# FNet and gated layers on one core: opening statistics moved between engines, two twin pairs for turning, and a stretch without tests

## The chip, the core and the metric

The kernel runs on one core of a Trainium2 chip. The metric is the device time of one execution in microseconds; the median of the runs counts. Engines are named as the profile names them: PE is TensorE's matmuls and PEld its weight loads, DVE is VectorE, ACT is ScalarE, POOL is GpSimd, SP is SyncE, whose queue issues nearly every DMA.

## The reference

Two rounds of two layers on x of 2048 rows and 640 columns. The first layer adds the real part of a two-dimensional DFT of the normalised rows, the second a gated product with hidden width 1728 (w_gate, w_up and w_down are drawn eight times larger than the function below it says):

```python
def _A_ref(x, dft_seq_re, dft_seq_im, dft_hid_re, dft_hid_im):
    a = jnp.einsum("bsd,ed->bse", x, dft_hid_re)
    b = jnp.einsum("bsd,ed->bse", x, dft_hid_im)
    return jnp.einsum("ts,bse->bte", dft_seq_re, a) - jnp.einsum("ts,bse->bte", dft_seq_im, b)
def _B_ref(x, w_gate, w_up, w_down):
    g = jnp.einsum("bsd,df->bsf", x, w_gate)
    u = jnp.einsum("bsd,df->bsf", x, w_up)
    return jnp.einsum("bsf,fd->bsd", _sigmoid(g) * u, w_down)
x = x + _A_ref(_layernorm(x), ...)
x = x + _B_ref(_layernorm(x), w_gate, w_up, w_down)
x = x + _A_ref(_layernorm(x), ...)
x = x + _B_ref(_layernorm(x), w_gate, w_up, w_down)
```

## The kernel before, in words

**The folded DFT.** The DFT matrices have mirror symmetry, and `folded` uses it: rows s and S-s, and s and S/2-s, are added and subtracted first, so that the sequence product is taken over a quarter of the rows. x stands in SBUF as four blocks (0 to 3) of four groups A, B, C, D of 128 rows; the groups B and C run backwards and have to be turned. `turn_round` (L349-352) does that on PE with a reversal matrix, two matmuls of 320 columns into a pair of PSUM banks called a twin; `turned` (L354-357) copies the twin back to SBUF on ACT and takes the sum of each row on the way. Four twins use all eight PSUM banks, and `drop_twins` gives these to the matmuls, as eight `acc` banks, once the last twin has been copied.

**Statistics.** The layer norm's mean and variance of each row come in two ways: by DVE's batch statistics (L415, L416), or on ACT. ACT's way is a sum, then a square of x minus the mean with the sum of the squares (`turned_squares`, L363-365, for B and C; `fold_stats_act`, L571-575, for five groups of A and D). For the square, POOL first makes the mean from the sum (`turned_means`, L361); afterwards POOL divides the squares' sum (`square_means`, L373), and `rstd_power` adds eps (L398) and takes the power -1/2 (L399), also on POOL. `rstd_step` (L401-408) then does a Newton step, in the opening on DVE, five small operations, and `fold_scale` (L600-613) makes the coefficients from it.

**Folds.** `fold_columns` (L578-585) adds and subtracts the column halves of a group pair on DVE, `fold_double` (L587-595) doubles column 0 (L590) and, for block 1, copies a single row (L595), `zero_odd` (L838-841) clears two columns, `fold_rows` (L615-630) scales the rows on ACT (L624, L626) and DVE (L630), and `fold_join` (L645-660) adds the four groups on DVE. `sequence32` (L802-822) is the first sequence DFT in fp32 on PE. A call takes its banks one after the other; `seq 0 1` stands first and has three chains.

**What sets the order.** Each engine runs its instructions in the order in which they are emitted. Until PE has its first down projection's operands, that order is the list `OPENING` (L156-178), written out by hand: "turn i g", "turned i g", "stats i g", "means i", "square i g", "smeans i", "power i", "scale i", "col i k", "double i k", "zero i", the row products "re", "ro", "de", "do", "join i e" and "join i o", "seq i tp", and so on, each word one call for block i (the dictionary `todo`, L1615-1645). Later the PE programme (`steps`) is run in order, each step with a planned duration; `when(t, f)` calls f at the planned time t, between steps. Memory is given out in slots by the table `PLACES` (L74-111), in the order in which it is taken.

**The second block of the gated layer.** Layer 0's rows are done in two halves. While PE runs the first half's down projection (L1299), the second half is normalised in four pairs of row tiles: ACT applies the norm (L442), DVE combines pairs (L492-495), ACT and DVE make f16 parts (L507, L508), and an SP transpose DMA (L524) turns them into PE's operand. The gate and up products (L1157) start when the last transpose has landed.

**Other work beside it.** The folding holds only if the DFT matrices have the symmetry. 100 tests check that while the layers run: each loads a tile of the matrix (L1485, mostly four DMAs on SP), compares on DVE (L1492, L1494) and sums squares on ACT (L1464); a flag sends the program to `general` if one fails. They are spread by `spans`: stretches of the plan with a weight, in which tests stand at even distances (4.704 planned us over the weight). Besides, `load_c`, `split_c` and `keep_c` (L702-730) load blocks of the DFT matrix again, split them into f16 parts (L236 on ACT, L238 on DVE) and store them for layer 1; L1059 to L1068 make sums of weights, and `load_s` (L1086 to L1092) loads the first products' weights.

## Time and profile before

| What | us |
|---|---|
| median of three runs (1130.19 to 1132.08) | 1131.68 |
| the profiled execution | 1127.54 |
| its span, first to last instruction | 1125.7 |
| PE busy in the span | 1089.4 |
| DVE busy | 834.2 |
| ACT busy | 571.7 |
| POOL busy | 153.7 |

The mean granted clock of the profiled execution was 0.988. The lines that matter are shown with the prediction. A line of the waits reads: engine, tile and line that waited, what released it, total us, times, longest. A line of the timeline reads: start, us, engine, line, operation, output from input and their shape, count, and in brackets the idle time before it with its releaser. A line of the groups reads: line, engine, operation, count, busy us, mean ns, and idle time before. A line of the windows gives for each engine the busy time and the count of instructions that started, then the granted clock of PE in parts of full speed and the mean busy share of the DMA engines.

### The profile page before, as it was taken

To read this page: it belongs to the slowest core of one execution; us is meant where nothing else is said; L and a number is where in the kernel's file an instruction comes from. 1 tells how busy PE (TensorE), PEld (TensorE's weight loads), DVE (VectorE), ACT (ScalarE), POOL (GpSimd) and SP (SyncE) were. 2 spreads that over 40 slices of the span, in tenths; PEclk is the share of its full clock that TensorE was granted. 3 is DMA by queue.
4 is the path that set the end of the run, shared out by engine and by line. 5 is a ranking of instruction groups with operands and counts; after the bars stand their busy time and mean duration, and the time that the engine had idled before them with its cause. 6 is when DMAs were issued, how large, how long until landed. Compare 5 with 4: busy or idle time off the path is not lost.

```text
span 1125.7 us, 17470 instructions
## 1 busy us (share of the span) xinstructions
PE 1089.4 (97%) x6279; PEld 621.4 (55%) x6279; DVE 834.2 (74%) x1623; ACT 571.7 (51%) x1108; POOL 153.7 (14%) x241
## 2 busy tenths in 40 slices
PE   5899999999997999999999999999999999999997
PEld 3667444447773444447777754444667444444775
DVE  7887589959385999858786659886796356767962
ACT  6776447856152556546224544477654245554520
POOL 3200131421322433100020100002000010000010
PEclk8899999999998999999999999999999999999999
DMA  8312674365989776856833027645668965655621
GB/s 280 140 36 69 189 231 148 124 187 165 232 226 293 254 212 226 235 172 201 239 87 133 1 47 180 191 148 172 203 158 175 232 220 176 224 184 179 201 84 62
DMA packets 183080, 194.69 MB, mean 173 GB/s; under 512 B 76459, under 2 KB 145476, under 8 KB 182984
## 3 DMA queue, kind: packets, MB, share of 16 engines
q1 hardware_dynamic: 182344, 190.86, 57.5%
q0 software_dynamic: 640, 2.62, 0.6%
q8 instruction: 51, 0.84, 0.3%
q14 instruction: 45, 0.37, 0.1%
HBM read 145.29 MB, written 31.90 MB: 157 GB/s over the span
## 4 chain that ended last, share of the span: by engine, by line
PE 79%; DVE 9%; DMA 4%; issue 3%; SPq 2%; POOL 2%; ACT 1%; DVEq 0%; POOLq 0%; ACTq 0%
PE acc L1157 39%; PE acc L1413 14%; PE acc L1113 14%; PE acc L907 4%; PE acc L819 2%; DMA big<-in_wu 2%; PE acc L1394 2%; PE acc L1266 2%; DVE big L238 1%; DMA big<-big 1%; DVE big L1287 1%; DVE big L508 1%; SPq L1485 1%; PE acc L776 1%; SPq L524 1%
## 5 line engine op out<-in xcount | busy, mean ns | idle before, releaser
L1157 PE MATMUL acc<-big 128*128 128x512 f16 x2160 | 469.0, 380 | 10.4 <-issue 7.9
L1157 PEld LDWEIGHTS <-big 128*128 128x128 f16 x2160 | 211.5, 98 | 266.6 <-issue 12.9
L1413 PE MATMUL acc<-big 128*128 128x320 f16 x1512 | 213.5, 299 | 2.5 <-DVE big L1287 2.5
L1161 ACT ACTIVATE big<-acc 128x512 f32<-128x512 f32 x160 | 94.2, 594 | 197.2 <-PE acc L1157 191.6
L1413 PEld LDWEIGHTS <-big 128*128 128x128 f16 x1512 | 147.9, 98 | 60.9 <-issue 3.1
L1113 PE MATMUL acc<-big 128*128 128x512 f16 (+1 forms) x900 | 156.3, 336 | 0.0
L1113 PEld LDWEIGHTS <-big 128*128 128x128 f16 x900 | 87.9, 98 | 67.6 <-issue 0.3
L1464 ACT ACTIVATE big<-big 128x768 f32<-128x768 f32 (+6 forms) x106 | 78.9, 745 | 51.7 <-DVE big L1494 21.2
L238 DVE SCALAR_TENSOR_TENSOR big<-big 128x640 f16<-128x640 f32 (+8 forms) x94 | 75.5, 826 | 26.1 <-ACT big L236 26.1
L1374 DVE TENSOR_TENSOR big<-big 128x512 f16<-128x512 f32 x126 | 84.5, 682 | 7.6 <-ACT big L1373 7.6
L1299 PE MATMUL acc<-big 128*128 128x320 f16 x656 | 89.3, 299 | 0.0
L1287 DVE SCALAR_TENSOR_TENSOR big<-acc,big 128x320 f32<-128x320 f32 x112 | 53.1, 484 | 42.6 <-PE acc L1394 24.6
L1373 ACT ACTIVATE big<-big 128x512 f16<-128x512 f32 x126 | 72.8, 617 | 18.6 <-DVE big L1251 7.9
L236 ACT ACTIVATE big<-big 128x640 f16<-128x640 f32 (+9 forms) x94 | 63.2, 706 | 30.9 <-DMA big<-in_ct 14.2
L1299 PEld LDWEIGHTS <-big 128*128 128x128 f16 x656 | 64.2, 98 | 25.1
L1207 DVE TENSOR_TENSOR big<-big,acc 128x512 f32<-128x512 f32 x40 | 27.2, 680 | 46.3 <-ACT big L1464 23.2
L1164 ACT ACTIVATE big<-big 128x512 f32<-128x512 f32 x80 | 49.7, 621 | 6.5 <-DVE big L1207 6.4
L507 ACT ACTIVATE big<-big 128x384 f16<-128x384 f32 (+2 forms) x56 | 36.5, 666 | 31.9 <-DVE big L492 17.1
L379 POOL DMA_INDIRECT out<-big,rows x8 | 9.0, 1121 | 312.0 <-DVE big L1287 164.8
L1385 DVE TENSOR_TENSOR big<-big 128x512 f32<-128x512 f32 x72 | 49.6, 691 | 0.1
L1492 DVE TENSOR_TENSOR big<-big 128x512 f32<-128x512 f32 x64 | 45.3, 707 | 4.6 <-DMA big<-in_ct 4.6
L907 PE MATMUL acc<-big 128*128 128x321 f16 (+3 forms) x324 | 48.5, 300 | 0.0
(193 smaller groups left out, 1196.0 us busy)
## 6 DMA issues: line engine op xcount, KB each, us to landing
big<-in_ct SPq DMA_DIRECT2D x256, 128.0 KB
big<-kept_f SPq DMA_DIRECT2D x63, 320.0 KB
big<-kept_S SPq DMA_DIRECT2D x33, 512.0 KB
big<-kept_w SPq DMA_DIRECT2D x33, 320.0 KB
big<-in_ct SPq DMA_DIRECT2D x32, 256.0 KB
big<-kept_G SPq DMA_DIRECT2D x21, 320.0 KB
kept_S<-big SPq DMA_DIRECT2D x13, 512.0 KB
big<-in_wg SPq DMA_DIRECT2D x19, 320.0 KB
```

Source lines behind the costliest of these rows:

```text
L236: nc.scalar.activation(dh, src, AF.Copy, scale=s)
L238: nc.vector.scalar_tensor_tensor(dl, src, s, dh, op0=OP.mult, op1=OP.subtract)
L907: nc.tensor.matmul(ps[:m, :EC], z[:, at : at + m], w[:, 384 * wp : 384 * wp + EC], start=(d == 0 and zp == HI and wp == HI), stop=(d == ND ...
L1113: nc.tensor.matmul(ps, w[wp][:, d * P : (d + 1) * P], xt[:, xp, :], start=(d == 0 and wp == HI and xp == HI), stop=(d == ND - 1 and wp == LO))
L1157: nc.tensor.matmul(ps, wt, xt, start=start and n == 0, stop=n == len(todo) - 1, skip_group_check=not start)
L1161: nc.scalar.activation(dst, ps, AF.Copy)
L1287: nc.vector.scalar_tensor_tensor(xe, ps[:, :EH], CB, xe, op0=OP.mult, op1=OP.add)
L1299: nc.tensor.matmul(held["pd", i, e][0][:, :EH], held["t", half, j].parts[hp][:, i * P : (i + 1) * P], held["w", 2, j].parts[wp][:, e * EH ...
L1373: nc.scalar.activation(h, v, AF.Copy)
L1374: nc.vector.tensor_tensor(l, v, h, op=OP.subtract)
L1413: nc.tensor.matmul(ps[:, :EH], a[n][hp][:, i * P : (i + 1) * P], w[n][:, wp], start=fresh and m == 0, stop=m == len(todo) - 1, skip_group_ ...
L1464: nc.scalar.activation(v, v, AF.Square, accum_out=new_sum()[:p])
```

## The change

It has five parts. Line numbers of the new kernel are one to five higher than those above.

1. **Who does the small operations of the opening.** ACT's squares take the raw sum as bias and -640 as scale, so they need no mean; the variance's factor becomes 1/D³ (`square_means`, now on DVE). POOL still makes the means, now also those of ACT's A and D groups. Adding eps goes from POOL to DVE and only the power stays on POOL; `rstd_step` on DVE has four operations for five. `fold_double` with its row copies goes from DVE to POOL while the opening lasts, and `zero_odd`'s memset too. Later, `norm_stats_act` is scaled in the same spirit, and `npow`'s eps goes to DVE.
2. **PSUM.** Two twins in place of four, one for B and one for C; the other four banks are `acc` banks from the start, and `drop_twins` adds four more.
3. **The list `OPENING`** is written anew, and with it the table `PLACES`.
4. **Tests.** The first span of the tests is split in two, with nothing between 38 and 76 us (of the plan) behind the start of layer 0's first down projection. With this the distance is 4.607 planned us over the weight.
5. **Layer 1's blocks of the DFT matrix** are loaded, split and stored from 96 planned us on, 11.5 apart, and no longer from 104 on, 13.5 apart.

```diff
 PLACES = """
-224 171 112 387 160 267 284 290 314 401 250 137 166 153 344 100 374 381 331 257 340 85 364 132 260 349 94 80
...
+305 80 399 324 195 319 369 208 352 246 286 400 130 100 81 105 125 153 269 121 156 374 346 273 262 143 116 159
...
 OPENING = """
-    turn 0 B, stats 0 A, turn 0 C, turned 0 B, turned 0 C, turn 1 B, stats 0 D, means 0, square 0 C, col 0 0,
-    turn 1 C, double 0 0, stats 1 A, turned 1 B, square 0 B, smeans 0, zero 0, col 0 1, turned 1 C, stats 1 D,
-    col 1 0, power 0, stats 2 D, turn 2 B, turned 2 B, turn 3 C, double 1 0, turn 2 C, double 0 1, col 1 1, means 1,
-    square 1 C, scale 0, col 2 0, wld 4 0, zero 1, re 0 0, turn 3 B, ro 0 0, turned 3 C, de 0 0, square 1 B,
-    double 1 1, ro 0 1, do 0 0, smeans 1, re 0 1, power 1, col 3 1, turned 2 C, stats 2 A, do 0 1, de 0 1, zero 2,
-    join 0 o, means 2, scale 1, join 0 e, double 2 0, square 2 C, ro 1 1, square 2 B, col 2 1, re 1 0, smeans 2,
...
+    turn 0 B, wld 4 0, stats 0 A, turned 0 B, turn 0 C, turn 1 B, square 0 B, turned 0 C, stats 0 D, col 0 0,
+    square 0 C, wld 3 0, means 0, col 0 1, smeans 0, turned 1 B, double 0 0, square 1 B, turn 1 C, zero 0, turn 2 B,
+    stats 1 D, turned 1 C, double 0 1, square 1 C, power 0, turn 2 C, col 1 0, turned 2 B, stats 1 A, means 1,
+    smeans 1, scale 0, double 1 0, stats 2 A, re 0 0, re 0 1, power 1, turned 2 C, ro 0 1, ro 0 0, stats 2 D,
+    col 1 1, square 2 B, turn 3 B, col 2 0, de 0 1, scale 1, square 2 C, de 0 0, do 0 0, col 2 1, row 0, zero 2,
+    smeans 2, means 2, turn 3 C, ro 1 0, join 0 e, ro 1 1, double 1 1, re 1 1, do 0 1, do 1 0, power 2, double 2 0,
...
     big = pool.tile([P, UNITS * UNIT], F32, name="big")
-    acc = []
+    psum = ctx.enter_context(tc.tile_pool(name="ps", bufs=1, space=bass.MemoryType.PSUM))
+    acc = [psum.tile([P, 512], F32, name=f"acc{i}") for i in range(4)]
     flag = pool.tile([P, 1], I32, name="flag")
...
     X = big[:, : XU * UNIT].rearrange("p (r c) -> p r c", c=D)
-    banks = []
+    banks = list(range(4))
     minus = pool.tile([P, 4], F32, name="minus")
...
     room_of = turning.__enter__()
-    twins = [room_of.tile([P, 2, 512], F32, name=f"twin{k}") for k in range(4)]
+    twins = [room_of.tile([P, 2, 512], F32, name=f"twin{k}") for k in range(2)]
...
     def twin(i, g):
-        return twins[(2 * i + (g == GC)) % 4]
+        return twins[g == GC]
...
     def drop_twins():
         turning.__exit__(None, None, None)
-        pool8 = ctx.enter_context(tc.tile_pool(name="ps", bufs=1, space=bass.MemoryType.PSUM))
-        acc.extend(pool8.tile([P, 512], F32, name=f"acc{i}") for i in range(8))
-        free_bank(*range(8))
+        rest = ctx.enter_context(tc.tile_pool(name="ps4", bufs=1, space=bass.MemoryType.PSUM))
+        acc.extend(rest.tile([P, 512], F32, name=f"acc{i}") for i in range(4, 8))
+        banks.extend(range(4, 8))
...
     def load_x(i, g):
...
-    def turned_means(i):
+    def sums_to_means(i):
         t = quad_tile(i)
-        nc.gpsimd.tensor_scalar(t[:, GB:GD, 12], t[:, GB:GD, 20], 1.0 / D, None, op0=OP.mult)
+        g0, g1 = GB - ((i, GA) in ON_ACT), GD + ((i, GD) in ON_ACT)
+        nc.gpsimd.tensor_scalar(t[:, g0:g1, 12], t[:, g0:g1, 20], 1.0 / D, None, op0=OP.mult)
...
     def turned_squares(i, g):
         t = quad_tile(i)
-        nc.scalar.activation(held["xr", i, g].f32, X[:, 4 * i + g, :], AF.Square, bias=t[:, g, 12:13], scale=-1.0,
+        nc.scalar.activation(held["xr", i, g].f32, X[:, 4 * i + g, :], AF.Square, bias=t[:, g, 20:21], scale=-float(D),
                              accum_out=t[:, g, 22:23])
...
         g0, g1 = GB - ((i, GA) in ON_ACT), GD + ((i, GD) in ON_ACT)
-        nc.gpsimd.tensor_scalar(t[:, g0:g1, 13], t[:, g0:g1, 22], 1.0 / D, None, op0=OP.mult)
+        nc.vector.tensor_scalar(t[:, g0:g1, 13], t[:, g0:g1, 22], 1.0 / D**3, None, op0=OP.mult)
...
     def store_x(i, g, c):
...
     def rstd_step(t, n, to, on=nc.gpsimd, times=-1.0):
...
         on.tensor_tensor(c[16], c[14], c[15], op=OP.mult)
-        on.tensor_tensor(c[17], c[16], c[15], op=OP.mult)
-        on.tensor_scalar(c[18], c[17], -0.5 * to, 1.5 * to, op0=OP.mult, op1=OP.add)
-        on.tensor_tensor(c[19], c[18], c[15], op=OP.mult)
         if on is nc.vector:
+            on.scalar_tensor_tensor(c[17], c[16], -0.5 * to, c[15], op0=OP.mult, op1=OP.mult)
+            on.scalar_tensor_tensor(c[19], c[17], 1.5 * to, c[15], op0=OP.add, op1=OP.mult)
...
         else:
+            on.tensor_tensor(c[17], c[16], c[15], op=OP.mult)
+            on.tensor_scalar(c[18], c[17], -0.5 * to, 1.5 * to, op0=OP.mult, op1=OP.add)
+            on.tensor_tensor(c[19], c[18], c[15], op=OP.mult)
             on.tensor_tensor(c[18], c[12], c[19], op=OP.mult)
...
     def norm_stats_act(r):
...
         t, junk = norm_t(r), take(5, "junk").f32
-        nc.scalar.activation(junk, X[:, r, :], AF.Copy, scale=1.0 / D, accum_out=t[:, 12:13])
-        nc.scalar.activation(junk, X[:, r, :], AF.Square, bias=t[:, 12:13], scale=-1.0, accum_out=t[:, 22:23])
-        nc.gpsimd.tensor_scalar(t[:, 13:14], t[:, 22:23], 1.0 / D, None, op0=OP.mult)
+        nc.scalar.activation(junk, X[:, r, :], AF.Copy, scale=D**-1.5, accum_out=t[:, 20:21])
+        nc.scalar.activation(junk, X[:, r, :], AF.Square, bias=t[:, 20:21], scale=-(D**-0.5), accum_out=t[:, 13:14])
+        nc.gpsimd.tensor_scalar(t[:, 12:13], t[:, 20:21], D**0.5, None, op0=OP.mult)
         drop("junk")
...
     def norm_stats_dve(r):
...
     def fold_stats_act(i, g):
...
         xg = X[:, 4 * i + g, :]
-        nc.scalar.activation(junk, xg, AF.Copy, scale=1.0 / D, accum_out=t[:, g, 12:13])
-        nc.scalar.activation(junk, xg, AF.Square, bias=t[:, g, 12:13], scale=-1.0, accum_out=t[:, g, 22:23])
+        nc.scalar.activation(junk, xg, AF.Copy, accum_out=t[:, g, 20:21])
+        nc.scalar.activation(junk, xg, AF.Square, bias=t[:, g, 20:21], scale=-float(D), accum_out=t[:, g, 22:23])
         drop("junk")
...
     def fold_columns(i, k):
...
     def fold_double(i, k):
...
         e, xg = folds(i)[0][:, g], X[:, 4 * i : 4 * i + 4, :][:, g]
-        nc.vector.tensor_scalar(e[:, :, EH:], xg[:, :, 0:1], 2.0, None, op0=OP.mult)
+        on = nc.vector if steps else nc.gpsimd
+        on.tensor_scalar(e[:, :, EH:], xg[:, :, 0:1], 2.0, None, op0=OP.mult)
         if i == SP:
...
                 take(6, "row")
-            nc.vector.tensor_copy(held["row"].f32[0:1, 384 * k : 384 * k + EC], e[0:1, 1])
+            on.tensor_copy(held["row"].f32[0:1, 384 * k : 384 * k + EC], e[0:1, 1])
...
     def fold_power(i, k0, k1, on=nc.gpsimd):
...
     def zero_odd(i):
...
-        nc.vector.memset(o[:, GB::2, EH:], 0.0)
+        nc.gpsimd.memset(o[:, GB::2, EH:], 0.0)
...
     def stored_c(r, i):
...
         todo = {
-            "turn": turn_round, "turned": turned, "means": turned_means, "square": turned_squares,
+            "turn": turn_round, "turned": turned, "means": sums_to_means, "square": turned_squares,
...
             "smeans": square_means,
-            "power": lambda i: fold_power(i, 0, 2), "scale": lambda i: fold_scale(i, 0, 2, nc.vector),
+            "power": lambda i: fold_power(i, 0, 2, nc.vector), "scale": lambda i: fold_scale(i, 0, 2, nc.vector),
             "col": fold_columns, "double": fold_double,
...
-            "npow": lambda p: rstd_power(norm_t(2 * p, 2), 2), "nscale": lambda p: rstd_step(norm_t(2 * p, 2), 2, XS, nc.vector),
+            "npow": lambda p: rstd_power(norm_t(2 * p, 2), 2, nc.vector), "nscale": lambda p: rstd_step(norm_t(2 * p, 2), 2, XS, nc.vector),
             "nrm": lambda r: norm_apply(r, r in APPLY_ACT),
...
                 for r in range(2):
-                    u = 104 + 13.5 * (2 * n + r)
+                    u = 96 + 11.5 * (2 * n + r)
                     when(u, load_c, r, n)
...
                     when(u + 7, stored_c, r, n)
-            when(104 + 3, load_c512)
-            when(104 + 6, split_c512)
-            when(104 + 8, stored_c512)
+            when(96 + 3, load_c512)
+            when(96 + 6, split_c512)
+            when(96 + 8, stored_c512)
             for j in range(5, NF):
...
         tests.insert(30 + 4 * n, test)
-    spans = [(start_of(0, "d", 0) + 6, start_of(0, "e"), 0.5),
+    spans = [(start_of(0, "d", 0) + 6, start_of(0, "d", 0) + 38, 0.4), (start_of(0, "d", 0) + 76, start_of(0, "e"), 0.55),
...
```

What the change moves is shown at three places. The first is POOL's queue in the opening; quad_67 to quad_70 hold the statistics of blocks 0 to 3 before, quad_74 to quad_77 after. Before:

```order
L361 TENSOR_SCALAR quad_67<-quad_67 128x2
L373 TENSOR_SCALAR quad_67<-quad_67 128x3
L398 TENSOR_SCALAR quad_67<-quad_67 128x4
L399 TENSOR_TENSOR quad_67<-quad_67,minus 128x4
L361 TENSOR_SCALAR quad_68<-quad_68 128x2
L373 TENSOR_SCALAR quad_68<-quad_68 128x2
L398 TENSOR_SCALAR quad_68<-quad_68 128x4
L399 TENSOR_TENSOR quad_68<-quad_68,minus 128x4
```

And of the new kernel:

```order
L363 TENSOR_SCALAR quad_74<-quad_74 128x3
L595 TENSOR_SCALAR big<-big 128x2
L846 MEMSET big 128x2
L595 TENSOR_SCALAR big<-big 128x2
L401 TENSOR_TENSOR quad_74<-quad_74,minus 128x4
L363 TENSOR_SCALAR quad_75<-quad_75 128x2
L595 TENSOR_SCALAR big<-big 128x2
L600 COPY big<-big 1x321
L401 TENSOR_TENSOR quad_75<-quad_75,minus 128x4
```

The square means and the additions of eps have left POOL; the doubles (L595), row copies (L600) and memsets (L846) have come between the means and the powers.

The second place is DVE's queue around block 0's joins (L660 before, L665 after), from which the first sequence product on PE takes its operand. Before:

```order
L660 TENSOR_TENSOR big<-big 128x320 x2
L403 TENSOR_TENSOR quad_68<-quad_68 128x4
L404 TENSOR_TENSOR quad_68<-quad_68 128x4
L405 TENSOR_SCALAR quad_68<-quad_68 128x4
L406 TENSOR_TENSOR quad_68<-quad_68 128x4
L408 SCALAR_TENSOR_TENSOR quad_68<-quad_68 128x4
L609 TENSOR_SCALAR quad_68<-quad_68,edge 128x2
L610 TENSOR_SCALAR quad_68<-quad_68,edge 128x4
L611 TENSOR_SCALAR quad_68<-quad_68,edge 128x2
L613 TENSOR_TENSOR coef_77<-quad_68 128x2
L660 TENSOR_TENSOR big<-big 128x321 x2
```

And of the new kernel, with its chains of blocks 0 and 1 done earlier:

```order
L635 SCALAR_TENSOR_TENSOR big<-big,quad_74 128x321
L635 SCALAR_TENSOR_TENSOR big<-big,quad_74 128x320
L588 TENSOR_TENSOR big<-big 128x2x320
L589 TENSOR_TENSOR big<-big 128x2x320
L375 TENSOR_SCALAR quad_76<-quad_76 128x4
L665 TENSOR_TENSOR big<-big 128x321 x2
L635 SCALAR_TENSOR_TENSOR big<-big,quad_74 128x320
L635 SCALAR_TENSOR_TENSOR big<-big,quad_75 128x320
L400 TENSOR_SCALAR quad_76<-quad_76 128x4
L665 TENSOR_TENSOR big<-big 128x320 x2
```

The scale of block 1 (L403 to L613) no longer stands between the two joins; a square mean, an addition of eps and a row product of block 1 do.

The third place is SP's queue between the second block's transposes (L524 before, L528 after). Before, from the first transpose to the second, and on to the loads behind it:

```order
L524 DMA_TRANSPOSE big<-big 128x34x128
L1485 DMA big<-in_ct 128x1x256 x4
L524 DMA_TRANSPOSE big<-big 128x34x128
L255 DMA kept_S_2672<-big 128x2048
L255 DMA kept_c_3_2674<-big 256x1x516
L1059 DMA big<-in_wg 128x640
L1059 DMA big<-in_wu 128x640
L709 DMA big<-in_ct 128x516
L1485 DMA big<-in_ct 128x1x256 x4
L255 DMA kept_S_2763<-big 128x2048
```

And of the new kernel, from the first transpose to the third:

```order
L528 DMA_TRANSPOSE big<-big 128x34x128 x2
L256 DMA kept_S_2657<-big 128x2048
L1064 DMA big<-in_wg 128x640
L1064 DMA big<-in_wu 128x640
L256 DMA kept_S_2737<-big 128x2048
L1064 DMA big<-in_wg 128x640
L1064 DMA big<-in_wu 128x640
L528 DMA_TRANSPOSE big<-big 128x34x128
```

Between the first and the last of the four transposes stood four tests' loads (16 DMAs), two stores and one load of the DFT blocks; now none of these does.

34 lines of the change are left out of this document (17 added, 17 removed), and 62 rows, old and new, of the table PLACES.

## The prediction

> **What bounds the kernel now.** I read the page's engine shares first, then TensorE's list of waits, then a table by stretches. Their lines:
>
> ```profile
> span 1125.7 us, 17470 instructions
> PE 1089.4 (97%) x6279; PEld 621.4 (55%) x6279; DVE 834.2 (74%) x1623; ACT 571.7 (51%) x1108; POOL 153.7 (14%) x241
> ```
> ```profile
> PE acc L819 <- ACT big L357: 7.9, 1, 7.9
> PE acc L1157 <- issue: 7.9, 1, 7.9
> PE twin L351 <- DVE big L307: 4.1, 1, 4.1
> PE twin L351 <- ACT big L575: 3.3, 1, 3.3
> PE acc L1413 <- DVE big L1287: 2.5, 3, 1.9
> PE acc L1157 <- DMA big<-big: 2.3, 1, 2.3
> PE twin L351 <- DMA big<-in_x: 1.4, 1, 1.4
> ```
>
> TensorE is busy for 97% of the span, and all its waits together (7.9 + 7.9 + 4.1 + 3.3 + 2.5 + 2.3 + 1.4 = 29.4 us) are what is left to win without fewer matmuls. The change issues the same matmuls. So its gain is what it takes out of these seven rows and the low clock behind them, its loss whatever new row it makes. The next table (PE busy, PEld, DVE, ACT, POOL, then the granted clock and the DMA share) says what the two long waits cost besides themselves:
>
> ```profile
> 31.50:36.60 5.10, 5.06 (x12) 3.63 (x13) 4.93 (x17) 4.86 (x11) 2.80 (x4) 0.50 1.03 405
> 36.70:84.50 47.80, 47.80 (x293) 30.93 (x293) 39.55 (x88) 32.55 (x67) 5.75 (x14) 1.00 0.11 37
> 340.00:343.80 3.80, 0.20 (x2) 0.00 (x0) 1.10 (x3) 0.00 (x0) 0.00 (x0) 1.00 1.06 281
> 343.90:350.60 6.70, 2.55 (x7) 0.91 (x8) 0.00 (x0) 0.00 (x0) 0.86 (x1) 0.50 1.05 268
> 878.00:885.00 7.00, 4.71 (x26) 2.30 (x25) 1.58 (x4) 1.60 (x4) 0.00 (x0) 1.00 0.70 183
> ```
>
> After the opening's wait, and again after the one that ends at 348.05, TensorE runs at a clock of 0.50; after the wait of 2.3 us near 880 it stays at 1.00. Behind 348.05 there are 2.55 us of work at half clock: about 2.55 / 2 = 1.3 us lost. Between 36.7 and 84.5 TensorE has no gap at all, though DVE idles 8 of 47.8 us, so work that starts earlier there can be followed by the folds.
>
> **First term: the opening.** TensorE's first sequence matmul is here, with what released it, and the copy of the last turned group on ScalarE:
>
> ```profile
> 31.54 5.83 PE L819 MATMUL acc<-big 128*128 128x256 f32 x14 [7.87 <-ACT big L357]
> ```
> ```profile
> 30.71 0.68 ACT L357 ACTIVATE big<-twin 128x640 f32<-128x640 f32 x1
> 31.30 0.19 ACT L357 ACTIVATION_READ_ACCUMULATOR big<-twin 128x1 f32 x1
> ```
>
> It started 0.05 us behind the copy's end (31.49), because all eight PSUM banks belonged to the turning. With four banks free from the start, `seq 0 1` (three banks) no longer needs that copy. What is late next is its operand, block 0's two joins on DVE (L660) and what stands ahead of them:
>
> ```profile
> 11.16 0.89 DVE L415 BATCH_NORM_STATS2 quad<-big 128x6 f32<-128x320 f32 x2 [0.97 <-DMA big<-in_x]
> ...
> 24.88 0.47 DVE L660 TENSOR_TENSOR big<-big 128x320 f32<-128x320 f32 x1
> 26.87 0.17 DVE L403 TENSOR_TENSOR quad<-quad 128x4 f32<-128x4 f32 x1 [1.52 <-POOL quad L399]
> ...
> 27.27 0.17 DVE L405 TENSOR_SCALAR quad<-quad 128x4 f32<-128x4 f32 x1
> ...
> 28.35 0.89 DVE L660 TENSOR_TENSOR big<-big 128x321 f32<-128x321 f32 x2
> ```
>
> The second join ended at 28.35 + 0.89 = 29.24. I counted what the new order puts ahead of it on DVE: the same six column pairs, three statistics and four row products of block 0; besides, three square means and three additions of eps (six tiny operations; the nearest, L405, takes 0.17, so 1.0 us) and one row product of block 1 (0.5); fewer are four doubles and two row copies (now GpSimd's), a scale's tail and the chain's fifth operation (together some 1.3). The net is about +0.2 us. Ahead of the joins DVE also idled 0.97 us for a load of x and 1.52 us for GpSimd's power of block 1. In the new order a column pair whose data is there stands at the first, and the power's squares on ScalarE take the raw sum, without waiting for GpSimd's means (one such wait is quoted below).
>
> With neither, the joins end at 29.24 - 0.97 - 1.52 + 0.2 = 26.95, and the first sequence matmul starts 4.6 us earlier; with both, at 29.4 + some 0.5 for a power that comes later than now, 1.6 us earlier. I take the middle row, the power's wait halved and the load's gone, with 0.5 us for handing over: **3.3 us** (bounds 1.6 and 4.6). The half clock behind it goes along with the start. The moves to GpSimd are hidden as long as its queue holds nothing up that DVE needs; what it costs if not is the third rival. `zero`, `wld 4 0` and `wld 3 0` I cost at nothing: the first is a memset that DVE ran beside other work, the others are one DMA issue each.
>
> [...] The rows first:
>
> ```profile
> 14.52 0.23 POOL L373 TENSOR_SCALAR quad<-quad 128x3 f32<-128x3 f32 x1 [2.53 <-ACT big L365]
> ...
> 22.00 3.44 POOL L373 TENSOR_SCALAR quad<-quad 128x2 f32<-128x2 f32 x1 [3.70 <-ACT big L365]
> ```
> ```profile
> 27.08 0.83 ACT L365 ACTIVATE big<-big,quad 128x640 f32<-128x640 f32 x1 [1.81 <-POOL quad L361]
> ```
>
> The operation took 0.23 us on three values, and 3.44 us on two; the long one ended at 25.44, 0.09 us behind a stretch in which DVE ran two-input operations without a gap (the L660 above ends at 25.35). [...]
>
> **Second term: the second block's transposes.** The wait that ended at 348.05 is named "issue", but a DMA transpose stands at its end. SP's queue and what follows:
>
> ```profile
> 299.75 2.62 SPq L1485 DMA_DIRECT2D big<-in_ct  x4
> 302.41 6.15 SPq L524 DMA_TRANSPOSE big<-big  x1
> ...
> 336.47 0.38 SPq L1086 DMA_DIRECT2D big<-kept_w  x1
> ...
> 338.46 7.28 SPq L524 DMA_TRANSPOSE big<-big  x1
> ```
> ```profile
> 348.05 4.25 PE L1157 MATMUL acc<-big 128*128 128x512 f16 x13 [7.86 <-issue]
> ```
> ```profile
> 311.94 0.92 ACT L442 ACTIVATE big<-big,rowt 128x640 f32<-128x640 f32 x1 [15.49 <-DMA big<-big]
> ```
> ```profile
> 334.12 0.95 DVE L508 TENSOR_TENSOR big<-big 128x768 f16<-128x768 f32 x1
> ```
>
> Read backwards: TensorE waits for the last transpose, issued at 338.46 (9.6 us to 348.05); that for the last parts on DVE (ending 335.07) and three loads in front of it in SP's queue; the parts for ScalarE's apply at 311.94, which waited 15.49 us for an earlier transpose, issued at 302.41 (9.5 us before), and that one stood behind four test loads. By the order, no test and no c store or load is left between the first and last of these transposes.
>
> Without the four loads the transpose of 302.41 is issued at 299.75: 2.66 us earlier, and ScalarE's apply with it. Then DVE is free of tests and of the c split (L238, 512 columns) between 311.94 and 335.07:
>
> ```profile
> L1494 DVE TENSOR_TENSOR big<-big 128x128 f32<-128x128 f32 x6 | 2.8, 513 | 0.1
> L1492 DVE TENSOR_TENSOR big<-big 128x512 f32<-128x512 f32 x3 | 2.6, 857 | 0.0
> ```
> ```profile
> 320.23 1.21 DVE L238 SCALAR_TENSOR_TENSOR big<-big 128x514 f16<-128x514 f32 x1
> ```
>
> That is 2.8 + 2.6 + 1.2 = 6.6 us out of a stretch in which these groups show no more than 0.1 us of idle time ahead of them. If all of it is on the chain, the parts end at 335.07 - 2.66 - 6.6 = 325.8; the three loads of weights in front of the transpose take 2.0 us (336.47 to 338.46), so it is issued between 325.8 and 327.8 and lands 9.6 us later, at 335.4 to 337.4. TensorE is ready at 348.05 - 7.86 = 340.2, or 336.9 once the opening has moved it by 3.3. What is left is 0 to 0.5 us, and I take 0.4: the wait falls by 7.86 - 0.4 = **7.5 us**, and the half clock behind it goes (**1.3**), since after the wait of 2.3 us there was none. If only half of DVE's 6.6 us is on the chain (ScalarE's parts and the evictions L1287 are the other legs), the transpose lands at 340.7, 3.8 us are left, the saving is 4.1 and the half clock may stay. So 4.1 to 9.2 us for the two together, 8.8 taken.
>
> **The tests that went elsewhere, the earlier c loads.** There are as many tests as before. Four or five leave the stretch and are spread over the rest, nearly all of it behind 340, where about 12% more run per microsecond. DVE has little room in part of it:
>
> ```profile
> 400.00:470.00 70.00, 70.00 (x325) 31.70 (x324) 68.30 (x115) 41.02 (x71) 22.60 (x26) 1.00 0.80 227
> ```
>
> A test costs DVE about 0.86 + 2 x 0.51 = 1.9 us at most (the means of the rows above), so one more in these 70 us fills DVE's 1.7 us of idle time. What DVE runs late there can be caught up in slacker stretches. I cost it at nothing, with 4 us (two tests that nothing hides) as the upper bound. The c loads are 8 to 20 us earlier, under matmuls that never waited for them: nothing. The waits of 2.5 and 2.3 us in layer 1 hang on a DVE eviction and a transpose with tests around them, whose places shift by less than a test's spacing: nothing, from 4 us less (both gone) to 4 more.
>
> **The sum.** 3.3 + 7.5 + 1.3 = 12.1 us. The profiled execution took 1127.54 us (span 1125.7, 1.8 us around it), so it would become 1115.4. It lies 4.1 us under the median of the three runs, 1131.68; against that, 1131.68 - 12.1 = 1119.6, and I forecast **1119.5 us**.
>
> **The rivals.** (a) *The opening only changes its wait.* GpSimd carries 17 reading operations up to block 3's power, as many as before, eight of them new, and a later power gives back what the banks bring: the second term alone, 1131.7 - 8.8 = 1122.9. For it: GpSimd's L373 of 3.44 us. Against it: what was slow there has left. Chance 0.17.
>
> (b) *The stall stays or comes back as DVE's.* If TensorE reaches 336.9 and the transposes land at 340.7, and DVE in 400 to 470 gives up another 2 to 4 us, the change is worth 3.3 + 4.1 - 3 = 4.4: about 1127.3. For it: DMA share 1.06 at 340, so transposes share the queues with loads that stay; DVE at 68.3 of 70. Against it: DMA share 0.11 to 0.8 elsewhere and DVE idle in the next stages (74% over the span). Chance 0.17.
>
> (c) *Slower: GpSimd's queue becomes the opening's bound.* From its first mean to its fourth power it ran 17 reading operations and some memsets; the first row has its busy time (the fifth) with all of them, 16.65 us, or 0.97 each for the 17 that read:
>
> ```profile
> 11.70:42.60 30.90, 18.59 (x54) 12.48 (x54) 27.77 (x79) 25.23 (x59) 16.65 (x24) 0.72 0.77 267
> ```
> ```profile
> L373 POOL TENSOR_SCALAR quad<-quad 128x4 f32<-128x4 f32 (+2 forms) x4 | 6.8, 1706 | 13.4 <-ACT big L365 13.4
> L361 POOL TENSOR_SCALAR quad<-quad 128x2 f32<-128x2 f32 x4 | 2.0, 499 | 0.1
> ```
>
> If each of the 17 of the new list takes the 1.7 us that L373 did, they need 28.9 us, 12.4 more, and DVE's scale operations wait for them: 1131.7 - 8.8 + 12.4 = 1135.3. It ends slower from a mean of (16.5 + 8.8) / 17 = 1.5 us on. Against it: L361, one short read like a double, took 0.5 on average, and DVE's new list has fewer two-input operations in a row. Chance 0.08.
>
> (d) *The change hardly acts* because the joins and the transposes' chain move by other legs (ScalarE): within 2 us of 1131.7. Chance 0.03.
>
> **How the numbers follow.** The forecast has 0.55. A measurement of this kernel can tell about 0.2% (2.3 us) from no change. (a) and nearly all of (b) are faster; of (b) 0.02 lies within 0.2% and 0.01 above. Faster 0.86, same 0.05, slower 0.09. The range takes in the forecast's bounds (best, 1131.7 - 4.6 - 9.2 - 4 = 1113.9, and 1.9 us more, by which the three runs of before differ: 1112) and, on the other side, (a) and (b), to 1128.5; (c) and (d) are left out with some of the tails.
>
> **What would show it.** The first L819 should start near 28.2 with no L357 as its releaser, but a DVE join; ScalarE's waits for L361 should be gone, and DVE should wait under 1 us for a power. No wait over 1.5 us should stand near 337, with the clock at 1.00 behind it, and the apply of the second pair should start 2 to 3 us earlier on ScalarE. I am wrong if TensorE waits in 37 to 85 for a fold, or for the second sequence matmul's banks (the last copy now frees those), if the last transpose lands more than 10 us behind its issue, or if DVE makes a wait in 400 to 470.

## The result, and the profile after

The new kernel takes 1118.12 us (median of four runs, 1116.7 to 1121.28) against 1130.93 for the kernel before on the same chip: a ratio of 0.9891, interval 0.9866 to 0.9916. A repeat beside later experiments gave 1118.91 against 1128.13, 0.9918 (0.9896 to 0.9941). The forecast was 1119.5. The profiled execution took 1118.15, 9.4 us less than that of before, and the terms below are read from this pair.

The first rows of the page of the new kernel, and TensorE's waits:

```profile
span 1116.3 us, 17439 instructions
PE 1090.2 (98%) x6279; PEld 620.7 (56%) x6279; DVE 827.8 (74%) x1608; ACT 570.8 (51%) x1108; POOL 157.6 (14%) x245
```
```profile
...
PE acc L824 <- POOL quad L363: 3.6, 1, 3.6
PE acc L1418 <- DVE big L1292: 2.5, 4, 1.2
PE acc L1418 <- DMA big<-kept_f: 2.5, 2, 2.3
...
PE acc L1162 <- DMA big<-big: 1.1, 1, 1.1
PE acc L1162 <- ACT big L1166: 1.0, 1, 1.0
PE acc L824 <- DVE big L665: 0.8, 1, 0.8
PE acc L1162 <- DVE big L1292: 0.7, 1, 0.7
```

Matmuls and PE's busy time are what they were. Of the two waits of 7.9 us, the second is now 0.7 (L1162), the first 3.6 and 0.8 (L824). New are 2.5 us for kept_f in layer 1's down projection (L1418), and 1.0 for an eviction (L1166), which was 0.2. The releaser in the row of 3.6 us, a mean on GpSimd, is only the one that ended nearest: what TensorE takes there are block 0's joins, and DVE's rows have their ends at 26.06 and 28.13, where its first two stretches begin:

```profile
25.18 0.88 DVE L665 TENSOR_TENSOR big<-big 128x321 f32<-128x321 f32 x2
...
27.25 0.88 DVE L665 TENSOR_TENSOR big<-big 128x320 f32<-128x320 f32 x2
```

How far TensorE is ahead is read where both kernels begin the same work: the first gate and up products (L1113, now L1118), then the first down projection (L1299, now L1304). TensorE's timeline, first of before, then of after, with the first sequence products and the second block's start as well:

```profile
84.54 55.64 PE L1113 MATMUL acc<-big 128*128 128x256 f16 x346
250.93 49.34 PE L1299 MATMUL acc<-big 128*128 128x320 f16 x362
```
```profile
26.16 1.19 PE L824 MATMUL acc<-big 128*128 128x256 f32 x2 [3.60 <-POOL quad L363]
28.18 10.94 PE L824 MATMUL acc<-big 128*128 128x256 f32 x36 [0.83 <-DVE big L665]
80.97 59.31 PE L1118 MATMUL acc<-big 128*128 128x256 f16 x363
248.31 51.91 PE L1304 MATMUL acc<-big 128*128 128x320 f16 x381
338.28 149.73 PE L1162 MATMUL acc<-big 128*128 128x512 f16 x693 [0.70 <-DVE big L1292]
560.44 2.60 PE L1418 MATMUL acc<-big 128*128 128x320 f16 x18 [0.30 <-DVE big L1292]
798.82 2.11 PE L1418 MATMUL acc<-big 128*128 128x320 f16 x12 [2.30 <-DMA big<-kept_f]
```

The lead is 84.54 - 80.97 = 3.57 us behind the opening. The start itself is 4.55 us earlier: 31.54 - 26.16, less the wait of 0.83 inside. Most of the difference is the clock. These windows, of before, then of after, have its mean in the two microseconds in which it rises from 0.50 to 1.00:

```profile
36.00:38.00 2.00, 2.00 (x9) 1.58 (x8) 2.00 (x6) 2.00 (x5) 0.00 (x0) 0.84 0.48 183
```
```profile
32.00:34.00 2.00, 2.00 (x7) 1.46 (x6) 2.00 (x5) 2.00 (x6) 0.00 (x0) 0.60 1.03 410
```

By them TensorE worked at half clock from 31.54 to 36.6 before, 5.1 us, and after in 26.16 to 33.6, 6.6 us without the wait. The 1.5 us more cost half of that, 0.7 us (an estimate from the clock of 0.50).

The lead is 2.62 us at the down projection, since the wait of 1.0 for L1166 lies between. It is 348.05 - 338.28 = 9.77 at the second block, and 11.0 at 560.44, against this row of before:

```profile
571.45 2.60 PE L1413 MATMUL acc<-big 128*128 128x320 f16 x18 [0.17 <-DVE big L1287]
```

The 1.24 us between 9.77 and 11.0 is the half clock that is gone, as this window of after shows (the clock follows the five busy times). Layer 1 gives 1.6 us back, mostly in the row of 798.82, and 9.4 are left.

```profile
336.00:345.00 9.00, 8.29 (x44) 3.98 (x43) 5.44 (x10) 3.60 (x7) 3.42 (x4) 1.00 0.85 247
```

### The profile page after: what moved, and what is told of

Read it like the earlier page. It is cut to its first block, busy times and chain, and to the rows that moved or that the text cites. A ratio compares the mean times of both kernels' runs of the same rounds, so it can differ in the third digit from the quotient of the medians.

```text
span 1116.3 us, 17439 instructions
## 1 busy us (share of the span) xinstructions
PE 1090.2 (98%) x6279; PEld 620.7 (56%) x6279; DVE 827.8 (74%) x1608; ACT 570.8 (51%) x1108; POOL 157.6 (14%) x245
## 3 DMA queue, kind: packets, MB, share of 16 engines
q0 software_dynamic: 640, 2.62, 0.6%
## 4 chain that ended last, share of the span: by engine, by line
PE 86%; DVE 7%; DMA 5%; ACT 1%; issue 1%; SPq 0%; DVEq 0%; POOL 0%; ACTq 0%; POOLq 0%
PE acc L1162 37%; PE acc L1418 14%; PE acc L1118 14%; PE acc L1304 8%; PE acc L912 4%; DMA big<-in_ct 2%; PE acc L824 2%; PE acc L1399 2%; PE acc L1271 2%; PE acc L781 1%; DMA big<-big 1%; DMA big<-in_x 1%; DVE big L1292 1%; DVE big L239 1%; DVE big L1379 0%
## 5 line engine op out<-in xcount | busy, mean ns | idle before, releaser
L1162 PE MATMUL acc<-big 128*128 128x512 f16 x2160 | 467.8, 379 | 2.8 <-DMA big<-big 1.1
L1162 PEld LDWEIGHTS <-big 128*128 128x128 f16 x2160 | 211.2, 98 | 258.1 <-issue 3.0
L1418 PE MATMUL acc<-big 128*128 128x320 f16 x1512 | 214.0, 299 | 5.1 <-DVE big L1292 2.5
L1418 PEld LDWEIGHTS <-big 128*128 128x128 f16 x1512 | 147.8, 98 | 64.3 <-issue 4.0
L1166 ACT ACTIVATE big<-acc 128x512 f32<-128x512 f32 x160 | 93.8, 592 | 168.6 <-PE acc L1162 168.2
L1118 PE MATMUL acc<-big 128*128 128x512 f16 (+1 forms) x900 | 156.3, 336 | 0.0
L1118 PEld LDWEIGHTS <-big 128*128 128x128 f16 x900 | 87.9, 98 | 67.6 <-issue 0.3
L1304 PE MATMUL acc<-big 128*128 128x320 f16 x656 | 89.3, 299 | 0.0
L1304 PEld LDWEIGHTS <-big 128*128 128x128 f16 x656 | 64.2, 98 | 25.1
L512 DVE TENSOR_TENSOR big<-big 128x384 f16<-128x384 f32 (+2 forms) x56 | 42.6, 774 | 8.4 <-ACT big L511 8.4
```

The lines of the kernel that those rows point to most:

```text
L1118: nc.tensor.matmul(ps, w[wp][:, d * P : (d + 1) * P], xt[:, xp, :], start=(d == 0 and wp == HI and xp == HI), stop=(d == ND - 1 and wp == LO))
L1162: nc.tensor.matmul(ps, wt, xt, start=start and n == 0, stop=n == len(todo) - 1, skip_group_check=not start)
L1166: nc.scalar.activation(dst, ps, AF.Copy)
L1304: nc.tensor.matmul(held["pd", i, e][0][:, :EH], held["t", half, j].parts[hp][:, i * P : (i + 1) * P], held["w", 2, j].parts[wp][:, e * EH ...
L1418: nc.tensor.matmul(ps[:, :EH], a[n][hp][:, i * P : (i + 1) * P], w[n][:, wp], start=fresh and m == 0, stop=m == len(todo) - 1, skip_group_ ...
```

## The experiments

All ratios are to the kernel before on the same chip.

**The stretch without tests.** Four kernels take the second term apart. The first puts four tests back, with all tests from layer 0's end on where they were. The spans are shown in short and with rounded weights; in the run a second list of spans places the tests alone, so that memory is taken at the same times as in the new kernel:

```diff
-(d0 + 6, d0 + 38, 0.4), (d0 + 76, start_of(0, "e"), 0.55)
+(d0 + 6, d0 + 38, 0.4), (d0 + 38, start_of(0, "e"), 0.4775)
```

> The new kernel with its test-free stretch filled again (four tests between 38 and 76 us of the plan, a weight of 0.478 behind it, so that all tests from layer 0's end on keep their places). If tests in SP's and DVE's queues made the second block's wait, the wait before its gate and up products comes back from 0.7 to 4 to 6 us with the half clock behind it, and the median rises by 4 to 7 us, to some 1123 to 1125. If the earlier loads of the DFT blocks took the wait away and the tests were hidden, the wait stays under 1.5 us and the median within 1 us of 1118.

Measured: 1130.05 us, ratio 1.0013 (1.0003 to 1.0023). The wait is longer than in either kernel:

```profile
347.27 152.63 PE L1162 MATMUL acc<-big 128*128 128x512 f16 x693 [10.59 <-DMA big<-big]
```

So the tests made the wait, and more than expected hangs on them: the opening's gain is lost too, because TensorE, which comes 3.5 us earlier (336.68 for 340.19), only waits longer for a last transpose that has come hardly earlier (its operand is there at 347.27 for 348.05). Then the two halves of a test, each alone. In `loads_only`, tests 1 and 2, loaded and not yet compared, are loaded two times more; in `dve_only`, the compares' shapes run on DVE, as maxima of a region with itself:

```diff
+for n, u in zip((1, 2, 1, 2), [40.1, 49.8, 59.4, 69.1]):
+    when(start_of(0, "d", 0) + u, within, n, tests[n][0], *tests[n][2])
```
```diff
+nc.vector.tensor_tensor(bd[:, :, 1], bd[:, :, 1], bd[:, :, 1], op=OP.max)
+for odd in range(2):
+    nc.vector.tensor_tensor(c[:, odd::2], c[:, odd::2], c[:, odd::2], op=OP.max)
...
+for u in [40.1, 49.8, 59.4, 69.1]:
+    when(start_of(0, "d", 0) + u + 1, dummy)
```

> The new kernel with only the DMAs of four tests in the stretch: two pending tests are loaded two times more, into the rooms that hold them. If SP's queue is the costlier half, the wait comes back as with whole tests, 4 us or more. If both halves count, as the prediction had it (2.7 us for the queue, 5.4 for DVE), it is 2 to 3.5 us. If only DVE counts, it stays under 1.5.

> The new kernel with only the DVE operations of four tests in the stretch (maxima of a region with itself, of the tests' shapes, no DMA and no squares). If both halves count, the wait is 2 to 4 us; if only the queue counts, it stays under 1.5 us and the median within 1 us of 1118.

Measured: 1128.38 us, ratio 1.0001 (0.9991 to 1.001), for the loads; 1117.62 us, 0.9901 (0.9884 to 0.9917), for DVE's operations. TensorE's row at the second block, loads first:

```profile
344.38 151.56 PE L1162 MATMUL acc<-big 128*128 128x512 f16 x693 [9.34 <-DMA big<-big]
```
```profile
336.89 149.73 PE L1162 MATMUL acc<-big 128*128 128x512 f16 x693 [0.84 <-DVE big L1292]
```

The loads alone bring the whole wait back, DVE's operations none of it. SP's queue, of the kernel with the loads, then of the new kernel, shows how:

```profile
307.59 2.62 SPq L1490 DMA_DIRECT2D big<-in_ct  x4
...
310.81 0.38 SPq L1064 DMA_DIRECT2D big<-in_wu  x1
...
323.49 5.19 SPq L528 DMA_TRANSPOSE big<-big  x1
...
329.35 2.58 SPq L1490 DMA_DIRECT2D big<-in_ct  x4
...
334.49 7.58 SPq L528 DMA_TRANSPOSE big<-big  x1
```
```profile
308.31 0.81 SPq L1064 DMA_DIRECT2D big<-in_wu  x1
...
320.61 5.16 SPq L528 DMA_TRANSPOSE big<-big  x1
...
329.76 6.75 SPq L528 DMA_TRANSPOSE big<-big  x1
```

A test's four loads hold SP's queue for 2.6 us. What stands behind them first is not a transpose but the weights for the sums on GpSimd (in_wg, in_wu). The sums wait for these, and ScalarE and DVE, each in order, wait for the sums before they come to the next pair of rows. GpSimd's first sum and ScalarE's next operation, with the loads and without:

```profile
316.60 0.73 POOL L1070 TENSOR_TENSOR big<-big 128x256 f32<-128x256 f32 x1 [14.68 <-DMA big<-in_wu]
```
```profile
318.05 0.42 ACT L237 ACTIVATE big<-big 128x256 f16<-128x256 f32 x1 [11.90 <-POOL big L1071]
```
```profile
313.73 0.73 POOL L1070 TENSOR_TENSOR big<-big 128x256 f32<-128x256 f32 x1 [12.89 <-DMA big<-in_wu]
```
```profile
315.18 0.42 ACT L237 ACTIVATE big<-big 128x256 f16<-128x256 f32 x1 [10.15 <-POOL big L1071]
```

All of it is 2.87 us later with the loads, and so is the third transpose (323.49 for 320.61). Another test's loads make it 4.73 at the last transpose (334.49 for 329.76). From there, TensorE gets its operand 9.9 us later with the loads, at most 8.5 (338.28) without. The rest of the wait, some 2.5 us, is that TensorE is ready earlier in this profile (335.0 for 337.6). DVE's operations alone cost little. In the new kernel DVE is idle for 10.00 us in that wait for the sums. With the operations the last transpose is issued 9.72 us behind the third (328.81 for 319.09), without them 9.15 (329.76 for 320.61), so it is only 0.57 us later: in the new kernel that transpose goes behind the loads of weights ahead of it in SP's queue, which end at 329.67, and not behind the parts, which end at 328.04.

The fourth kernel is the one before, with the test-free stretch alone (again a second list, for the tests only):

```diff
-spans = [(start_of(0, "d", 0) + 6, start_of(0, "e"), 0.5),
+spans = [(d0 + 6, d0 + 38, 0.5), (d0 + 76, start_of(0, "e"), 0.5759),
```

> The kernel before, with the test-free stretch alone (38 to 76 us of the plan, a weight of 0.576 behind it up to layer 0's end; all else as it was, the late splits of the DFT blocks too). If the tests made the wait, it falls from 7.9 us to 1 to 3 us (1.2 us of it for the split that stays on DVE, and the opening is not earlier), and the median falls by 5 to 8 us, to 1123 to 1126. If the DFT blocks' loads made it, it stays at 6 us or more.

Measured: 1119.28 us, ratio 0.9911 (0.9894 to 0.9928), 9.2 us less than before. TensorE doesn't wait at the second block (it changes over at 341.11 without a gap), although its opening is as it was and the splits of the DFT blocks stay:

```profile
341.11 19.16 PE L1157 MATMUL acc<-big 128*128 128x512 f16 x88
```

This one line of the change brings all that the intervals show of the whole change (0.9866 to 0.9916, and 0.9896 to 0.9941 in the repeat).

**The opening.** `four_twins` gives the new kernel back its four twins, with no `acc` bank before the last copy:

```diff
-banks = list(range(4))
+banks = []
...
-return twins[g == GC]
+return twins[(2 * i + (g == GC)) % 4]
...
```

> The new kernel with four twins again and no bank free before the last copy. If the banks are what lets the first sequence matmul go early, it waits for the last turned copy (29.9 in the new kernel's trace) and TensorE loses about 3 us against it (its first chain now starts at 26.2 with 0.8 us of waiting inside, as if at 27.0 without): some 1121. If the gain of the opening comes from the statistics alone, the start stays at 27 to 28 and the time within 1 us of 1118.

Measured: 1119.43 us, ratio 0.9915 (0.9898 to 0.9932), which its interval doesn't separate from the new kernel. The profile does (its execution took 1122.56, the longest of the four):

```profile
29.80 10.31 PE L823 MATMUL acc<-big 128*128 128x256 f32 x38 [10.26 <-ACT big L357]
```
```profile
81.95 58.23 PE L1117 MATMUL acc<-big 128*128 128x256 f16 x358
```

It waits for the copy, as expected. The new kernel starts 2.8 us earlier (26.16, and 0.83 of waiting inside), but is only 1.0 us ahead at the gate and up products (1.9 ahead in the profile of the repeat, 80.01). Again it is the clock: here TensorE worked for 3.1 us at half clock, for 6.6 in the new kernel. So of the 4.55 us of earlier start, 2.8 are the banks' and 1.7 the new list's and the statistics'; how much of each is left behind the half clock differs by profile.

That half clock explains nearly the whole spread of the openings. From the first sequence matmul to the gate and up products, less TensorE's waits and less half of its time at 0.50, 13 of the 14 profiles, those of all kernels but `joins_first` below, have 50.4 to 50.8 us (the clock read in windows of 0.25 us), while the time at 0.50 goes from 3.1 to 7.0 us. The clock rose 3.1 to 7.9 us after the first of these matmuls. What sets that moment was not tried.

`raw_sums_in_before` takes the squares' part alone:

```diff
-AF.Square, bias=t[:, g, 12:13], scale=-1.0
+AF.Square, bias=t[:, g, 20:21], scale=-float(D)
...
```

> The kernel before, with squares on ScalarE that take the raw sum (means on GpSimd for all groups of ScalarE, those of block 3 behind its last sum); its list, its banks and who does what are kept. If ScalarE's waits for the means hold the last turned copy up, the copy and the first sequence matmul come 1.5 to 2 us earlier (29.5 to 30 for 31.54) and the median falls by as much. If the turning itself (TensorE's waits for its operands) sets the copy, the start stays within 0.5 us.

Measured: 1128.59 us, ratio 1.0006 (0.9992 to 1.002), and a start at 31.46 for 31.54. ScalarE's 4.5 us of waiting for the means are gone, but it now waits for others, and the copy ends where it did (31.40 for 31.49):

```profile
ACT big L575 <- DMA big<-in_x: 5.8, 2, 3.2
ACT big L627 <- DVE quad L407: 2.1, 2, 1.6
```

The raw sums bring nothing in the old list; alone they only change the wait.

`doubles_on_dve` and `means_on_gpsimd` undo who does what:

```diff
-on = nc.vector if steps else nc.gpsimd
+on = nc.vector
...
```
```diff
-nc.vector.tensor_scalar(t[:, g0:g1, 13]
+nc.gpsimd.tensor_scalar(t[:, g0:g1, 13]
...
-"power": lambda i: fold_power(i, 0, 2, nc.vector)
+"power": lambda i: fold_power(i, 0, 2)
```

> The new kernel with the doubles, row copies and zeroing of the opening back on DVE. If DVE's queue ahead of the joins is the bound, as the prediction counted it, its second join ends some 1.3 us later (four doubles of 0.16 and two copies of 0.32) and the whole by as much, about 1119.4. If GpSimd's reads hold DVE up or are held up by it, so that moving them there cost what it saved, the joins end no later than now.

> The new kernel with the square means and the additions of eps of the opening back on GpSimd. If these operations are stretched there beside a busy DVE (1.7 us on average for a square mean before), the powers come 1.5 to 3 us later, DVE waits for them and TensorE starts 1 to 2.5 us later. If DVE's list now leaves the powers enough time (0.8 and 1.7 us are free behind the first two), the start moves by less than 0.5 us.

Measured: 1121.49 us, 0.994 (0.9923 to 0.9956), and 1118.6 us, 0.9915 (0.9894 to 0.9937). The gate and up products begin at 80.75 and 80.47. The seven profiles with the new kernel's opening have it between 79.00 and 81.20, so neither moves it by more than the profiles differ. With the means on GpSimd nothing is lost, as the second reading had it. With the doubles on DVE TensorE goes on 0.65 us later behind the second join (28.83 for 28.18), half of what was counted; the seven profiles have 27.04 to 28.45 there, so that is hardly more than they differ. Its time is 2 to 3 us above the new kernel's, clear of the first measurement's interval, though not of the repeat's. The profile shows no more than a longer wait for kept_f in layer 1 (3.2 us for 2.3); the cause is left open.

**Layer 1's new wait.** The kept_f loads that TensorE waits for at 798.82 stand in SP's queue behind tests, one of which loads rows of the small DFT matrix (in_wh):

```profile
777.45 1.94 SPq L1550 DMA_DIRECT2D big<-in_wh  x2
779.44 4.18 SPq L1046 DMA_DIRECT2D big<-kept_w  x2
783.72 8.92 SPq L1490 DMA_DIRECT2D big<-in_ct  x8
792.73 1.52 SPq L1366 DMA_DIRECT2D big<-kept_f  x3
```
```profile
SPq L1490 <- DMA big<-in_wh: 4.0, 2, 2.6
```

SP's test loads waited 4.0 us for the landing of in_wh, and everything behind them in the queue with them.

Two kernels were run beside the unchanged one (the first edit moves the small matrix's tests in the list, the second changes two weights, rounded here):

```diff
-tests.insert(30 + 4 * n, test)
+tests.insert(30 + 4 * n if n < 6 else 48 + 3 * n, test)
```
```diff
-(start_of(1, "j", 0, JC), start_of(1, "d", 0), 1.0), (start_of(1, "d", 0), start_of(1, "j", 1, 0), 0.4)
+(start_of(1, "j", 0, JC), start_of(1, "d", 0), 1.27), (start_of(1, "d", 0), start_of(1, "j", 1, 0), 0.1)
```

> The new kernel unchanged, to have it on the same chip as the two below: a ratio to before near 0.989, a wait near 2.3 us for kept_f at the first product of layer 1's down projection, and between 0.3 and 1 us before the second block's gate and up products.

> The new kernel with the sixteen tests of the small DFT matrix (the loads named in_wh) put elsewhere in the list of tests, so that none stands at the start of layer 1's down projection. If the tests' loads that wait 4.0 us in SP's queue for such a load hold the stage's kept_f loads up, the wait of 2.3 us goes and the median falls by 1.5 to 2.5 us against the unchanged kernel. If it is the number of loads there, the wait stays at 1.5 us or more.

> The new kernel with a weight of 0.1 for 0.4 in the stretch of layer 1's first down projection (about two tests for seven; the others go to the stretch before it). If loads in SP's queue make the wait for kept_f there and DVE's tests the waits of 1.2 and 0.4 us behind it, 2.5 to 4 us go and the median falls as much against the unchanged kernel. If the queue is late already when the stretch begins (the tests ahead of it now being denser), the wait stays or grows.

Measured: 1118.91 us (0.9918, 0.9896 to 0.9941) unchanged, 1115.99 (0.9889, 0.9865 to 0.9914) with the small matrix's tests moved, 1135.95 (1.0062, 1.0038 to 1.0087) with few tests. Moved, the kept_f loads are issued at 791.40 for 792.73, and the wait is gone from that profile. The intervals overlap, so the time alone doesn't show it, and TensorE is itself 2 us later there in this profile (562.32 for 560.44), behind a wait of 2.78 us and a half clock at the second block (693 matmuls in 151.31 us for 149.73). In the next kernel, with the same tests and TensorE no later, 0.57, 0.24 and 0.15 us of the wait are left. So most of it was the in_wh tests'. The other kernel shows the price of density: the tests that left the stretch make the one ahead of it too dense, and the same loads come far later.

```profile
PE acc L1418 <- DMA big<-kept_f: 10.9, 1, 10.9
```

**A list with the joins first**, together with the moved tests (the list's changed part, without its line breaks):

```diff
-de 0 0, do 0 0, col 2 1, row 0, zero 2, smeans 2, means 2, turn 3 C, ro 1 0, join 0 e, ro 1 1, double 1 1, re 1 1, do 0 1, do 1 0, power 2, double 2 0, re 1 0, join 0 o, turned 3 C
+de 0 0, do 0 0, join 0 e, do 0 1, join 0 o, col 2 1, row 0, zero 2, smeans 2, means 2, turn 3 C, ro 1 0, ro 1 1, double 1 1, re 1 1, do 1 0, power 2, double 2 0, re 1 0, turned 3 C
```

> The kernel with the moved tests of the small matrix, and besides the opening's list changed so that block 0's second join no longer stands behind a column pair of block 2 and three row products of block 1 on DVE. If the joins set TensorE's start, both joins end near 25.8 (they end at 28.1 in the new kernel), the first sequence matmul goes then without a wait inside, and 1.5 to 2.4 us are won: a ratio of about 0.987, where the moved tests alone had 0.989. If an earlier start is eaten behind it (block 1's joins end near 32.5 as they did, or the two banks of the second product wait for the last copies), the start is earlier, but TensorE waits again before 45 and less than 0.7 us are won.

Measured: 1113.81 us, ratio 0.9867 (0.985 to 0.9883), the fastest of all. Its interval lies under the repeat's (0.9896 to 0.9941 for `after_again`), but overlaps the first measurement's (0.9866 to 0.9916). TensorE's rows:

```profile
24.79 1.19 PE L824 MATMUL acc<-big 128*128 128x256 f32 x2 [1.68 <-issue]
26.14 10.15 PE L824 MATMUL acc<-big 128*128 128x256 f32 x31 [0.15 <-DVE big L665]
80.28 59.96 PE L1118 MATMUL acc<-big 128*128 128x256 f16 x366
```

The joins do set the start, which is 2.0 us earlier (26.14 for 28.18). But the gate and up products begin at 80.28, within the spread of the others: the earlier start is eaten before them, as the second reading had it. Here it isn't the half clock (5.8 us of it): the stretch that has 50.4 to 50.8 us elsewhere takes 52.3, and 1.0 us of that lies between 41 and 51, where 38 matmuls take 9.7 us for 8.7 at a clock of 1.00. What holds these up is open. Its margin over the moved tests alone is not separated by the intervals; the two profiles differ most at the second block (a wait of 0.76 us for 2.78), which this list doesn't touch.

## Why the prediction was right

**Sum and signs.** The terms were 3.3 for the opening, 7.5 for the wait at the second block, 1.3 for the half clock, and nothing for the rest: 12.1 in all. The profiles have 3.57 (2.62 by the down projection), 7.16, 1.24, and 1.6 us lost in layer 1: 9.4 in all. So each term had its sign and nearly its size, but the sum was 2.7 us too large: from the profile of before it gave 1115.4, and 1118.15 was measured. The forecast of 1119.5 came near because it started from the median of 1131.68, 3 us above what the kernel before took in all later runs (medians 1128.08 to 1128.48). That is luck.

**The opening.** The start at 28.2 behind a DVE join came as predicted for all but the first two matmuls (26.16), and L361's waits on ScalarE and the power's wait on DVE are gone. DVE's list was the bound, as counted: its joins ended at 28.1. Two of the term's parts were off and nearly cancel: the wait for a load of x, taken as gone, is still there (0.85 us for 0.97), and the wait for the power, taken as halved, is gone. The first two matmuls needed only the first join, so the start is 4.55 us earlier and not 3.3. But an earlier start isn't a gain of the same size: 4.55 us became 3.57, and 2.8 (`four_twins`) and 2.0 us (`joins_first`) became 1.0 and 0.7. "The half clock behind it goes along with the start" was wrong: TensorE worked 6.6 us at half clock for 5.1. That the gain came out near 3.3 is partly luck. The term's 0.5 us for handing over is shown by no run: TensorE's first two matmuls began 0.10 us behind the first join's end (26.06 to 26.16), the next 0.05 behind the second's (28.13 to 28.18). In the runs' times the opening isn't seen at all: `gap_in_before`, without it, has 0.9911, the whole change 0.9891 and 0.9918.

**The transposes: right in size, wrong in one step.** The step that failed is what the last transpose waited for: "that for the last parts on DVE (ending 335.07) and three loads in front of it in SP's queue", and with it "That is 2.8 + 2.6 + 1.2 = 6.6 us out of a stretch ... If all of it is on the chain". The parts were not the last to come. From the end of the third transpose (329.23) SP's queue in the kernel before ran to the last one without a pause of more than 0.1 us, and 6.0 us of this are the loads of two tests, which have no term in my sum; it counted 2.66 us, for the loads ahead of the second transpose. Before, then `gap_in_before`:

```profile
324.01 5.22 SPq L524 DMA_TRANSPOSE big<-big  x1
329.28 3.01 SPq L1485 DMA_DIRECT2D big<-in_ct  x4
...
332.89 2.97 SPq L1485 DMA_DIRECT2D big<-in_ct  x4
```
```profile
321.45 5.20 SPq L524 DMA_TRANSPOSE big<-big  x1
326.70 1.54 SPq L255 DMA_DIRECT2D kept_S<-big  x2
...
331.22 6.58 SPq L524 DMA_TRANSPOSE big<-big  x1
```

Without the tests the last transpose goes 7.2 us earlier (331.22 for 338.46): the third is 2.6 us earlier, and the other 4.7 come behind it, where the two tests' loads stood. In the new kernel the loads alone bring the whole wait back, and the tests' operations on DVE make the last transpose 0.57 us later against the third (`dve_only`). My reading went from the transpose to DVE's operations and missed what stood in the same queue, for the transpose and for GpSimd's sums. For the kernel before, the share of DVE was not tried alone. The apply of the second pair came not 2 to 3 us earlier but 12.7 (299.27 for 311.94); in `gap_in_before` it came 3.5 earlier (308.45), and the wait was gone as well, so that step was not the bound.

**The rest.** "Nothing, from 4 us less to 4 more" held as a range: the tests' new places met kept_f's loads. That 12% more tests run per microsecond holds, by the weights, only up to layer 0's end; behind it they are 2% denser. DVE in 400 to 470 was busy for 64.0 us, not more than the 68.3 of before.

**The rivals.** (a) fell by the profiles, 3.57 us for the opening; by the times alone, as said, it is not excluded. (b) fell: 0.7 us are left (1.78 in the repeat's profile, still at full clock behind it: 149.73 us for the same 693 matmuls). (c) fell: DVE waits for no power. ScalarE does wait 1.7 us for a row copy on GpSimd, which I hadn't counted. Of the new operations on GpSimd the doubles took 251 ns on average:

```profile
L595 POOL TENSOR_SCALAR big<-big 128x2 f32<-128x2 f32 x8 | 2.0, 251 | 0.0
```

Seven of the eight ran almost wholly while DVE was idle, took a tile's statistics or worked on a few values. The one that ran beside two-input operations (at 26.14) took 0.47 us. The prediction's short row of 0.23 us, too, stood beside statistics (L415 and L416, to 14.81). With the doubles on DVE GpSimd's four powers took 2.53 us on average, for 1.49 in the new kernel. What makes these operations longer at times was not tried alone. The opening's gain, 3.57 us, stayed above its lower bound of 1.6.

## What to carry to other kernels

Where one queue issues nearly all DMAs in order, look at what stands behind a transfer that isn't urgent before you look at its compute: four loads of 0.65 us each delayed weights, sums, two engines' queues and a transpose. A gain upstream is worth nothing while such a chain sets the date downstream (`tests_back` has the whole new opening and a ratio of 1.0013), so remove the later wait first. And of moved work ask where it becomes dense: the same tests cost nothing, the whole gain, or 17 us, by their place.

## What the runs showed of the hardware

A test's four DMAs took 2.6 us of SP's queue in many places (2.62 at 307.59 in `loads_only`), 6.42 at 810.65 in the kernel before, and a transpose of layer 0's second block 5.2 to 8.8 (5.16 in the new kernel, 8.79 in `tests_back`). Seven profiles with one opening differ by 2.2 us at the same matmul (79.00 to 81.20), more than most edits of the opening move it; the time that TensorE works at a clock of 0.50 behind the turning, 4.2 to 7.0 us in these seven, makes 1.1 us between the earliest and the latest, and the start 1.2. With the doubles on DVE, GpSimd's powers took 2.53 us on average, for 1.49 in the new kernel; the cause was not tried.
